# First batch's scores as float32 products from q and k, two heads in the rows' halves, and four pairs with float32 values instead of five

## The chip, the cores and the metric

The kernel runs on one core of one Trainium2 chip. The metric is device time in microseconds, the median of several executions. Engines are named as the profile names them: PE (TensorE matmuls), PEld (its weight loads), DVE (VectorE), ACT (ScalarE), POOL (GpSimd), and SP, whose queue issues the DMAs.

## The reference

Attention with a decay, and then a feed-forward layer, all in float32:

```
scores = q @ k.T / 8 + cum[query] - cum[key]      # cum: running sum of log f; causal mask
attn   = exp(scores - max);  attn /= sum(attn) + 1e-9
x      = attn @ v            # 8 batches, 8 heads, 576 positions, 64 wide
h      = x @ w_in;  out = (h * tanh(softplus(h))) @ w_out      # 4608 tokens, 512 -> 2048 -> 512
```

## The kernel before, in words

Two heads make a pair; there are 8 batches of 4 pairs, 32 pairs `g`. A chunk of the feed-forward layer takes 512 tokens: chunk `c` below 8 the first 512 positions of batch `c`, the ninth the 64 last positions of all batches. So the first chunk needs pairs 0 to 3 and, as it goes, the converted weights: `load_weights`, `convert_weights`, `scale_weights` and `split_weights` bring 32 blocks of w_in and w_out in and split each into an f16 high and low half.

Precision comes from such halves. `prep` (line 1060) scales q and k of a pair by a power of two found from their square sums (`square_sum`, on ACT), makes high halves (`scaled`) and low halves (`scaled_rest`) into a tile `hl`, and moves them by DMA into a stacked layout: `ST1` holds the 64 high rows of a head and under them six rows of decay sums with ones as partners, `ST2` high and low rows of the cross terms (`prep2`, line 1094). The constant rows of `ST1` are written at the start by `fill_rows` (line 755). A score is then two f16 products of up to 128 rows added in a PSUM bank. The decay sums are made once by `decay` (line 782) in three f16 parts, stored to DRAM (`cumd`) and read back for each pair.

Pairs below `NB` = 5 go one way, the later pairs another.

- Pairs 0 to 4: `max_items` makes the scores with queries as PSUM rows, from `ST1` alone, and DVE takes maxima of tiles; `fin` turns them by a transpose into rows `mr` (for pairs below `NSEL` = 4; pair 4 stores them into a row of `ST1` by DMA). `st_items` makes the scores again with keys as PSUM rows, in two passes, adds a mask product and, for pairs below 4, a product of a selector `sel` with `mr` that subtracts the maximum; ACT takes the exponential into f32 tiles. `pv_items` multiplies these by the f32 values `vf`, which hold a column of ones; `prep_v` scales v into them.
- Later pairs: `new_st_items` makes the scores once, with queries as rows, DVE adds the mask and finds the maximum, ACT takes the exponential, `turn` splits it into f16 halves (copy on ACT, difference on DVE) and turns them by a DMA transpose, and `new_pv_items` multiplies by f16 halves of v, three products a block.

Every operation is recorded in a `Program`, with `choose` where several engines could do it, and `beside` where products in different parts of the array go out together. `schedule` then lays down the order of each engine's queue from a cost for each operation (`cost`, line 262; `F32COL` for f32 products) and the dependences; `warmed` puts products into an unused bank where TensorE would be idle early. In the trace all of them stand under the line that records (L333), so rows are told apart by tiles and shapes. PSUM has seven banks for attention until pair 3 is done, then two.

Of the kernel before, what the change touches and what calls it, by code (L numbers as in the profile page):

```python
# [33 lines left out]
EXPMASK = 0x7F800000  # L34
LEAST = float(np.array([963 << 20], np.uint32).view(np.float32)[0])
KM = 71
MROW = 70
# [26 lines left out]
NSEL = 4  # L64
# [37 lines left out]
NB = 5  # L102
# [25 lines left out]
VTA = -1  # L128
# [32 lines left out]
class Program:  # L161
# [100 lines left out]
    def cost(self, eng, method, kw, aps):  # L262
# [421 lines left out]
def attn_moe(ctx: ExitStack, tc: tile.TileContext, qk, v, f, w_in, w_out, out):  # L684
# [7 lines left out]
    sp = Ring(ctx.enter_context(tc.tile_pool(name="sp", bufs=1)), pt=CH, hb=CH, me=CH, ot=CH)  # L692
# [54 lines left out]
    rowv = cp.tile([P, 2, 2], F16, name="rowv")  # L747
    for t, first, fills in ((0, 0.0, ((KM - 4, -1.0), (KM - 1, 0.0))), (1, 1.0, ((KM - 4, 0.0), (MROW, -MSC), (KM, 0.0)))):
        nc.gpsimd.memset(rowv[:, t], first)
        for row, x in fills:  # L750
            nc.gpsimd.affine_select(
                out=rowv[:, t], in_=rowv[:, t], pattern=[[0, 2]], compare_op=ALU.is_ge, fill=x,
                base=row - 1, channel_multiplier=-1)

    def fill_rows(t, e):
        for k in range(2):
            rows = t[D:P, :, k].bitcast(F32)
            one = ones[D:P, 0:96].unsqueeze(1).to_broadcast([D, 3, 96])
            for j in range(2):
                nc.choose(scaled(  # L760
                    rows[:, j].rearrange("p (a n) -> p a n", n=96), one, rowv[D:P, k].bitcast(F32), e))

    for t in ST1:
        fill_rows(t, "vector" if t is ST1[0] else "scalar")
# [5 lines left out]
    xat = xa[2]  # L770

# [10 lines left out]
    def decay():  # L782
# [8 lines left out]
        nc.vector.tensor_scalar(out=c[:, 0], in0=cm, scalar1=8.0, scalar2=None, op0=ALU.mult)  # L791
        nc.vector.scalar_tensor_tensor(
            out=r1, in0=cm, scalar=8.0, in1=c[:, 0], op0=ALU.mult, op1=ALU.subtract)
# [27 lines left out]
    def square_sum(o, x, scale=1.0):  # L821
        junk = sp.tile([P, S], BF16, name="junk", tag="junk", bufs=1)
        nc.scalar.activation(
            out=junk[:, 0 : x.shape[-1]], in_=x, func=AF.Square, scale=scale, accum_out=o)
# [22 lines left out]
    def all_sum(cols, name, least=2.0**-60):  # L847
        m = sp.tile([P, 1], F32, name="am_m", tag="am_m", bufs=4)
# [131 lines left out]
    def load_v(b, after=-1):  # L980
        vt[b] = []
        for p in range(NP):
            t = sp.tile([P, S], F32, name=f"v{b}_{p}", tag="v32", bufs=NV)
            if after >= 0:

                nc.gpsimd.tensor_copy(out=t[:, 0:1], in_=st[after]["hl"][:, 3, 0:1])
            nc.sync.dma_start(out=t, in_=v[b, p])
            vt[b].append(t)

    def amax_v(b):  # L990
        cols = sp.tile([P, NP], F32, name=f"vc{b}", tag="vc", bufs=4)
        for p in range(NP):
            square_sum(cols[:, p : p + 1], vt[b][p])
# [53 lines left out]
    def load_qk(g):  # L1047
        b, p = divmod(g, NP)
        if g in (2, 3):
            t = xa[(2, 0)[g - 2]].rearrange("p a h n -> p (a h n)").bitcast(F32)[:, 0 : 2 * S]  # L1050
# [6 lines left out]
    def place1(g):  # L1057
        return g % NST if g < NB else (g - NB + ((NB - 1) % NST == 0)) % 2

    def prep(g):  # L1060
        b, p = divmod(g, NP)
# [13 lines left out]
        if g in (1, 3):  # L1075
            hl = xa[1].rearrange("p a h n -> p (a h n)")[:, 0 : 4 * S].rearrange("p (t s) -> p t s", t=4)
        else:
            hl = sp.tile([P, 4, S], F16, name=f"hl{g}", tag="hl", bufs=NHL)
# [6 lines left out]
        nc.mark = f"rows{g}" if g < NSEL else None  # L1085
        for t in range(2):
            nc.sync.dma_start(out=ST1[i][D + 3 * t : D + 3 * t + 3, :, t], in_=cumd[h0 : h0 + 2].rearrange("h r s -> r h s"))
        nc.mark = None
        for j in range(2):
            nc.sync.dma_start(out=ST1[i][0:D, j], in_=hl[j * D : (j + 1) * D, 1:3])  # L1090
        if NSEL <= g < NB and g - NST >= NSEL:
            nc.sync.dma_start(out=ST1[i][MROW : MROW + 1, :, 0], in_=zrow[0:1])

    def prep2(g):
        hl = st[g]["hl"]
# [5 lines left out]
    def prep_v(g):  # L1101
        b, p = divmod(g, NP)
        vv = sp.tile([P, 9 * (D + 1)], F32, name=f"vv{g}", tag="vv")
        src = vt[b][p].rearrange("p (n d) -> p n d", d=D)
        if g < NB:
            vf = st[g]["vf"] = vv.rearrange("p (n d) -> p n d", d=D + 1)
            nc.gpsimd.memset(vf[:, :, D : D + 1], 1.0)
            nc.choose(*(scaled(vf[:, :, 0:D], src, vsc[b], e) for e in ("scalar", "vector", "gpsimd")))
            return
# [11 lines left out]
    if NB > NSEL + NST:  # L1121
        zrow = cp.tile([1, 2, S], F16, name="zrow")
        nc.gpsimd.memset(zrow, 0.0)

# [3 lines left out]
    def beside(*products):  # L1128
# [6 lines left out]
    sel = more_e.rearrange("p a n -> p (a n)").bitcast(F16)[:, 0 : 9 * P].rearrange("p (t k) -> p t k", t=9)  # L1135
    nc.vector.tensor_scalar(
        out=sel, in0=idm[:, 0:9].unsqueeze(2).to_broadcast([P, 9, P]), scalar1=-MSC / 1024.0, scalar2=None,
# [3 lines left out]

    def max_items(g):

        q1, k1 = ST1[place1(g)][:, :, 0], ST1[place1(g)][:, :, 1]
        s = st[g]
        KX = P

        def begin():

            s["mx"] = sp.tile([P, 20], F32, name=f"mx{g}", tag="mx", bufs=4)  # L1150
            nc.gpsimd.memset(s["mx"][:, 0:8:4], -3e38)

        def qk(o, j, t, k0, n, stop=True):
            q0 = t * P
            mm(o, q1[0:KX, j, q0 : min(q0 + P, S)], k1[0:KX, j, k0 : k0 + n], True, stop)
# [5 lines left out]
        def masked(c, ps, a, n, mb):  # L1161
            if g < GM:
                red(c, ps.rearrange("p (a n) -> p a n", a=a), a)
            else:
                d = sp.tile([P, a, n], F32, name=f"dg{g}_{c}", tag="ot", bufs=NOT)
                nc.vector.tensor_tensor(
                    out=d, in0=ps.rearrange("p (a n) -> p a n", a=a),
                    in1=mb.unsqueeze(1).to_broadcast([P, a, n]), op=ALU.add)
                red(c, d, a)

        def diag(j):
            ps = bank(f"md{j}_{g}")
            for t in range(4):
                qk(ps[:, t * P : (t + 1) * P], j, t, t * P, P, g >= GM)
                if g < GM:
                    mm(ps[:, t * P : (t + 1) * P], idm, msk, False, True)
            masked(10 + 4 * j, ps, 4, P, mskb)

        def t31(j):
            ps = bank(f"mt31{j}_{g}")  # L1180
            qk(ps[:, 0:384], j, 3, 0, 384)
            qk(ps[:, 384:512], j, 1, 0, 128)
            red(4 * j + 3, ps[:, 0:384])
            red(4 * j + 1, ps[:, 384:512])

        def t2():
            ps = bank(f"mt2_{g}")
            for j in range(2):
                qk(ps[:, 256 * j : 256 * j + 256], j, 2, 0, 256)
# [807 lines left out]
```

## Time and profile before

| | |
|---|---|
| median of 3 runs | 1017.91 us (1016.69 to 1018.59) |
| span of the profiled execution | 1012.6 us |
| the profiled execution's own time | not stated by the page; the median is 5.3 us above the span |
| PE, DVE, ACT busy | 978.1, 731.1, 728.9 us (97, 72, 72%) |
| chain that ended last | PE 65%, DVE 16%, ACT 7%, DMA 6% |

A busy PE is the union of its products' times, and the products are pipelined, so busy time is not work at the peak rate; what one product costs in a full queue is read from the distance between two starts. Each f32 product appears as two records.

### The profile page before, as it was taken

The numbers are of one execution on the slowest core, as the hardware profiler recorded it, in microseconds if no ns is written. First come the engines' busy times: TensorE is split into PE (matmuls) and PEld (weight loads), VectorE is DVE, ScalarE is ACT, GpSimd is POOL, SyncE is SP. The second block draws the span as 40 slices with busy tenths as digits, with TensorE's granted clock in tenths as the row PEclk, the third lists the DMA queues.
The fourth block names the chain that finished last, engine by engine and source line by source line (L and its number), as shares of the span: only waits on it lengthen the run. The fifth ranks groups of instructions, "written<-read, shape, count | busy, mean of one in ns | idle before, by whom it ended". The sixth has DMA issues, their size and how long they took to land.

```text
span 1012.6 us, 20652 instructions
## 1 busy us (share of the span) xinstructions
PE 978.1 (97%) x7663; PEld 544.1 (54%) x7663; DVE 731.1 (72%) x2002; ACT 728.9 (72%) x1421; POOL 10.4 (1%) x65
## 2 busy tenths in 40 slices
PE   4999899998999999999999999999999999999998
PEld 4788445544554554555455555455555555656664
DVE  7999999986677776776666766776766669953432
ACT  6668999978778777777778877787886665524323
POOL 2000000000000000000000000000000000000000
PEclk8999999999999999999999999999999999999999
DMA  6999974779777857687868766786775432001001
GB/s 198 324 266 244 262 169 108 154 173 187 158 145 160 173 127 153 136 180 145 142 141 179 148 146 142 170 158 115 138 152 112 70 75 72 4 1 42 1 1 42
DMA packets 256446, 139.57 MB, mean 138 GB/s; under 512 B 226650, under 2 KB 227034, under 8 KB 256346
## 3 DMA queue, kind: packets, MB, share of 16 engines
q1 hardware_dynamic: 256346, 138.26, 61.7%
q8 instruction: 60, 0.98, 0.4%
q14 instruction: 40, 0.33, 0.1%
HBM read 45.68 MB, written 9.66 MB: 55 GB/s over the span
## 4 chain that ended last, share of the span: by engine, by line
PE 65%; DVE 16%; ACT 7%; DMA 6%; issue 3%; SPq 1%; POOL 0%; DVEq 0%; ACTq 0%; POOLq 0%
PE b L333 65%; DVE wall L333 3%; DVE b L333 2%; DMA pt<-hb 2%; DMA st<-hl 2%; SPq L333 1%; ACT junk L333 1%; DVE hl L333 1%; DVE hb L333 1%; ACT st L333 1%; ACT hb L333 1%; DMA out_dram<-ot 1%; DVE gl L333 1%; DVE x L333 1%; ACT more_e L333 1%
## 5 line engine op out<-in xcount | busy, mean ns | idle before, releaser
L333 PEld LDWEIGHTS <-wall 128*128 128x128 f16 x3372 | 322.3, 98 | 357.9 <-issue 24.0
L333 PE MATMUL b<-gh,wall 128*128 128x512 f16 x1152 | 366.5, 380 | 0.0
L333 PE MATMUL b<-xa,wall 128*128 128x512 f16 (+1 forms) x1602 | 345.0, 366 | 8.3 <-ACT me L333 4.6
L333 PE MATMUL b<-gl,wall 128*128 128x512 f16 x576 | 218.2, 379 | 0.6 <-DVE gl L333 0.6
L333 PE MATMUL b<-st 70*128 70x512 f16 (+11 forms) x918 | 139.1, 285 | 13.7 <-DMA st<-cumd 6.9
L333 DVE SCALAR_TENSOR_TENSOR gl<-me,gsc,gh 128x512 f16<-128x512 f32 x144 | 106.3, 748 | 32.6 <-ACT gh L333 31.7
L333 ACT ACTIVATE me<-b,cinv 128x512 f32<-128x512 f32 (+1 forms) x130 | 85.0, 660 | 56.6 <-PE b L333 55.7
L333 PEld LDWEIGHTS <-st 70*128 70x128 f16 (+3 forms) x1110 | 87.3, 102 | 63.6 <-issue 18.7
L333 PE MATMUL b<-vv,pt 128*128 128x65 f16 (+5 forms) x2548 | 111.7, 203 | 1.1 <-DMA pt<-hb 0.7
L333 DVE CUSTOM_DVE_ANT_0 b<-b,mskw 128x256 f32<-128x256 f32 (+2 forms) x162 | 91.6, 567 | 9.9 <-PE b L333 8.8
L333 ACT ACT_TABLE_LOAD x70 | 89.8, 1283 | 1.2
L333 PEld LDWEIGHTS <-pt 128*128 128x128 f16 (+1 forms) x2268 | 70.9, 101 | 19.3 <-DMA pt<-hb 2.3
L333 ACT ACTIVATE st<-b,mn 128x512 f32<-128x512 f32 (+3 forms) x120 | 62.1, 548 | 22.7 <-DVE mn L333 19.4
L333 DVE TENSOR_TENSOR hb<-st,hb 128x512 f16<-128x512 f32 x81 | 55.8, 689 | 29.6 <-ACT hb L333 29.1
L333 DVE TENSOR_TENSOR hb<-more_e,hb 128x512 f16<-128x512 f32 x81 | 55.5, 689 | 29.6 <-ACT hb L333 29.3
L333 ACT ACTIVATE more_e<-b,mn 128x512 f32<-128x512 f32 (+3 forms) x123 | 62.4, 539 | 17.3 <-DVE mn L333 15.8
L333 DVE TENSOR_SCALAR gh<-me,gsc 128x512 f16<-128x512 f32 x66 | 31.9, 483 | 45.2 <-ACT me L333 44.3
L333 ACT ACTIVATE gh<-me,gsc 128x512 f16<-128x512 f32 x78 | 55.8, 720 | 1.8
L333 ACT ACTIVATE hb<-more_e 128x512 f16<-128x512 f32 x81 | 50.1, 627 | 9.5 <-DMA pt<-hb 8.8
L333 ACT ACTIVATE hb<-st 128x512 f16<-128x512 f32 x81 | 50.2, 627 | 7.6 <-DMA pt<-hb 5.6
L333 DVE TENSOR_TENSOR me<-b,hb 128x256 f32<-128x256 f32 x42 | 17.5, 422 | 50.5 <-PE b L333 49.9
L333 ACT ACTIVATE junk<-qk 128x576 bf16<-128x576 f32 x60 | 40.8, 680 | 15.5 <-DMA qk<-in_qk_dram 14.8
(173 smaller groups left out, 1005.3 us busy)
## 6 DMA issues: line engine op xcount, KB each, us to landing
st<-hl SPq DMA_DIRECT2D x180, 144.0 KB
qk<-in_qk_dram SPq DMA_DIRECT2D x30, 576.0 KB
v<-in_v_dram SPq DMA_DIRECT2D x32, 288.0 KB
out_dram<-ot SPq DMA_DIRECT2D x36, 256.0 KB
wall<-in_w_in_dram SPq DMA_DIRECT2D x16, 512.0 KB
wall<-in_w_out_dram SPq DMA_DIRECT2D x16, 512.0 KB
pt<-hb SPq DMA_TRANSPOSE x162
st<-xa SPq DMA_DIRECT2D x12, 144.0 KB
```

The costliest lines, as they stand in the source:

```text
L333: r = getattr(real[eng], method)(*a, **kw)
```

## The change

`NB` goes from 5 to 4, so pair 4 takes the later pairs' way. For pairs 0 to 3 there are no halves of q and k any more: the products take the loaded f32 q and k, whose two heads lie in rows 0 to 63 and 64 to 127, and put both heads' products side by side, each into a bank of its own. The decay term comes from `rk`, a tile with three rows of sums for each head, multiplied by ones; masks and maxima are added as f16 products of half height. For the 64 last queries of the maxima, `qz` holds q of both heads on the diagonal of a 128 x 128 block, and one product of full height does both. v is loaded straight into the f32 value tiles beside a ones column, unscaled; its scale moves into the reciprocal of the sums. `prep2`, `prep_v`'s scaling, `fill_rows` and the third `ST1` tile go.

The diff, cut to its core:

```diff
-KM = 71
-MROW = 70
+KR = D + 3
-NSEL = 4
-NB = 5
+NB = 4
...
                 m = int(out.shape[0])
-                n = max(F32COL * n * m / 128.0, 2.1 * m)
+                n = max(F32COL * n * m / 128.0, 2.1 * m) if rows > D else 4.2 * n
                 active = 0.44 * n
...
-    NST = 3
-    ST1 = [cp.tile([P, 2, 2, S], F16, name=f"st1_{i}") for i in range(NST)]
+    ST1 = [cp.tile([P, 2, 2, S], F16, name=f"st1_{i}") for i in range(2)]
...
-    for t in ST1:
-        fill_rows(t, "vector" if t is ST1[0] else "scalar")
+    rk = cp.tile([P, NB, S], F16, name="rk")
+    nc.gpsimd.memset(rk.rearrange("p g s -> p (g s)").bitcast(F32), 0.0)
...
     def load_v(b):
...
+            if b * NP + p < NB:
+                tag, n = ("v32", NV) if p < 2 else ("vv", 2)
+                t = sp.tile([P, 9 * (D + 1)], F32, name=f"v{b}_{p}", tag=tag, bufs=n)
+                t = t.rearrange("p (n d) -> p n d", d=D + 1)
+                nc.gpsimd.memset(t[:, :, D : D + 1], 1.0)
+                nc.sync.dma_start(out=t[:, :, 0:D], in_=v[b, p].rearrange("k (n d) -> k n d", d=D))
...
+    def prep_first(g):
+        h0, x = 2 * g, st[g]["qk"]
+        k = rk[:, g]
+        nc.mark = f"rows{g}"
+        for j in range(2):
+            nc.sync.dma_start(out=k[j * D : j * D + 3], in_=cumd[h0 + j])
+        nc.mark = None
+        z = qz(g)
+        for j in range(2):
+            r = slice(j * D, (j + 1) * D)
+            nc.gpsimd.tensor_copy(out=z[r, r], in_=x[r, 0, CH:S])
+
     def prep(g):
+        if g < NB:
+            prep_first(g)
+            return
...
     def max_items(g):
...
+        def scores(o, t, k0, n, tri=False):
+            q = slice(t * P, (t + 1) * P)
+            beside(*((o[j], x[r, 0, q], x[r, 1, k0 : k0 + n], True, False) for j, r in enumerate(HEADS)))
+            if tri:
+                for h in range(2):
+                    beside(*((o[j], (idm, idmx)[j ^ h][r], (msk, mskx)[j ^ h][r], False, False)
+                        for j, r in enumerate(HEADS)))
+            beside(*((o[j], one16[r], k[r, k0 : k0 + n], False, True) for j, r in enumerate(HEADS)))
...
         def t4a():
             ps = bank(f"mt4a_{g}")
-            for j in range(2):
-                qk(ps[j * D : (j + 1) * D], j, 4, 0, CH)
+            mm(ps, z, x[:, 1, 0:CH], True, False)
+            mm(ps, blk, k[:, 0:CH], False, True)
             red(8, ps)
...
     def st_items(g):
...
+        def block(o, k0, m, q0, n, tri=0):
+            ks = slice(k0, k0 + m)
+            beside(*((o[j], x[r, 1, ks], x[r, 0, q0 : q0 + n], True, False) for j, r in enumerate(HEADS)))
+            if tri and m == P:
+                for h in range(2):
+                    beside(*((o[j][:, h * D : (h + 1) * D], (msk, mskx)[j ^ h][r], idm[r, r], False, False)
+                        for j, r in enumerate(HEADS)))
+            elif tri:
+                beside(*((o[j], msk[r, r], idm[r, r], False, False) for j, r in enumerate(HEADS)))
+            for q in range(q0, q0 + n, P):
+                w = min(P, S - q)
+                tail = q == CH
+                beside(*((
+                    o[j][:, q - q0 : q - q0 + w], sel[r, 8 if tail else 4 * j + q // P, 0:m],
+                    s["mr"][r, r if tail else slice(0, P)], False, False)
+                    for j, r in enumerate(HEADS)))
+            ones_n = one16[:, 0 : min(n, P)]
...
+            beside(*((o[j], k[r, ks], ones_n[r], False, True) for j, r in enumerate(HEADS)))
...
+        def k2_():
+            ps = two("2")
+            block([o[:, 0:256] for o in ps], 2 * P, P, 2 * P, 256, P)
             for kt in range(4):
-                two_pass(ps[:, 256 + D * kt : 320 + D * kt], j, slice(kt * P, (kt + 1) * P), slice(CH, S))
-            finish(ps, f"T2{j}", CH, lambda e: tri(e, 1, P))
+                block([o[:, 256 + D * kt : 320 + D * kt] for o in ps], kt * P, P, CH, D)
+            finish(ps, "T2")
```

## Rows read from the trace of the kernel before

**Rows 1.** Stretches: length, busy (count) of PE, PEld, DVE, ACT, POOL, clock, DMA share.

```profile
0.00:20.00 20.00, 8.43 (x104) 8.19 (x105) 15.20 (x40) 14.27 (x29) 5.50 (x34) 0.88 0.57 180
20.00:40.00 20.00, 16.32 (x179) 12.35 (x176) 17.59 (x44) 11.21 (x25) 0.24 (x1) 0.87 0.99 310
40.00:100.00 60.00, 58.99 (x648) 50.13 (x648) 59.29 (x173) 45.54 (x114) 0.81 (x4) 1.00 1.00 266
100.00:200.00 100.00, 94.89 (x702) 48.58 (x701) 99.02 (x287) 97.53 (x174) 0.81 (x4) 0.98 0.75 174
...
300.00:500.00 200.00, 197.25 (x1597) 101.02 (x1596) 137.69 (x387) 153.62 (x298) 1.11 (x8) 1.00 0.75 154
860.00:1000.00 140.00, 140.00 (x902) 88.03 (x900) 70.92 (x146) 52.56 (x95) 0.00 (x0) 1.00 0.03 9
```

**Rows 2.** Groups of PE by form, 0 to 40 us: busy us, mean ns.

```profile
L333 PE MATMUL b<-idm,idh 128*128 128x128 f16 x133 | 12.2, 253 | 4.6 <-DVE idh L333 4.6
```

**Rows 3.** Waits up to 200 us: total, times, longest.

```profile
PE b L333 <- DMA st<-cumd: 6.9, 1, 6.9
```

**Rows 4.** Timeline of the opening: start us, length us, instruction.

```profile
2.02 1.79 DVE L333 TENSOR_SCALAR st<-ones,rowv 64x288 f32<-64x288 f32 x4 [0.36 <-POOL rowv L333]
2.09 3.48 ACT L333 ACTIVATE st<-ones,rowv 64x288 f32<-64x288 f32 x8
...
8.29 0.68 ACT L333 ACTIVATE junk<-qk 128x576 bf16<-128x576 f32 x1
...
11.00 0.71 SPq L333 DMA_DIRECT2D cumd<-st  x2
...
14.22 1.05 SPq L333 DMA_DIRECT2D st<-cumd  x3
...
18.51 0.27 PE L333 MATMUL b<-st 128*128 128x128 f16 x1 [6.94 <-DMA st<-cumd]
...
19.56 1.35 DVE L333 TENSOR_REDUCE mx<-b 128x4 f32<-128x512 f32 x3 [1.36 <-PE b L333]
```

**Rows 5.** Timeline of PE at full clock: merged products of one form.

```profile
38.11 0.33 PE L333 MATMUL b<-mr,more_e 128*128 128x128 f16 x3
...
39.40 1.53 PE L333 MATMUL b<-vv,pt 128*128 128x65 f32 x12
...
44.73 0.28 PE L333 MATMUL b<-vv,evs 128*64 128x65 f32 x2
...
44.94 0.23 PE L333 MATMUL b<-st 128*64 128x64 f16 x2
45.10 0.44 PE L333 MATMUL b<-vv,pt 128*128 128x65 f32 x2
...
57.66 0.36 PE L333 MATMUL b<-wsc,ones 128*128 128x4 f32 x2
...
338.60 0.57 PE L333 MATMUL b<-vv,pt 128*64 128x65 f16 x24
...
870.04 0.59 PE L333 MATMUL b<-gh,wall 128*128 128x512 f16 x2
```

**Rows 6.** Groups of PE by form, whole span.

```profile
L333 PE MATMUL b<-vv,pt 128*128 128x65 f32 x240 | 31.5, 277 | 0.0
```

**Rows 7.** Groups of DVE by form, 20 to 200 us.

```profile
L333 DVE SCALAR_TENSOR_TENSOR hl<-qk,qt,hl 128x576 f16<-128x576 f32 x10 | 8.0, 804 | 0.0
L333 DVE TENSOR_TENSOR hb<-more_e,hb 128x512 f16<-128x512 f32 x10 | 6.9, 688 | 0.0
L333 DVE TENSOR_REDUCE mx<-b 128x4 f32<-128x512 f32 x10 | 6.8, 679 | 1.5 <-PE b L333 1.5
```

**Rows 8.** Groups of ACT by form, 20 to 200 us.

```profile
L333 ACT ACTIVATE junk<-qk 128x576 bf16<-128x576 f32 x12 | 8.1, 679 | 1.1 <-DMA qk<-in_qk_dram 1.0
...
L333 ACT ACTIVATE hl<-qk,qt 128x576 f16<-128x576 f32 x7 | 5.3, 768 | 0.8 <-DMA st<-cumd 0.5 <-DVE qt L333 0.3
```

**Rows 9.** DMA issues, 0 to 100 us: count, KB of one.

```profile
st<-hl SPq DMA_DIRECT2D x25, 144.0 KB
```

More of the change, by code (lines that the diff above doesn't have):

```diff
@@ L34 @@
 EXPMASK = 0x7F800000
+ONE2 = float(np.array([0x3C003C00], np.uint32).view(np.float32)[0])
 LEAST = float(np.array([963 << 20], np.uint32).view(np.float32)[0])
-KM = 71
-MROW = 70
+KR = D + 3
 MSC = 2.0**10
@@ L738, in attn_moe @@
     nc.vector.memset(ones, 1.0)
-    NST = 3
-    ST1 = [cp.tile([P, 2, 2, S], F16, name=f"st1_{i}") for i in range(NST)]
+    ST1 = [cp.tile([P, 2, 2, S], F16, name=f"st1_{i}") for i in range(2)]
     ST2 = [cp.tile([P, 2, 2, S], F16, name=f"st2_{i}") for i in range(NST2)]
[L747 to L758, printed above, removed]
-            for j in range(2):
-                nc.choose(scaled(
-                    rows[:, j].rearrange("p (a n) -> p a n", n=96), one, rowv[D:P, k].bitcast(F32), e))
+    rk = cp.tile([P, NB, S], F16, name="rk")
+    nc.gpsimd.memset(rk.rearrange("p g s -> p (g s)").bitcast(F32), 0.0)
     for t in ST1:
-        fill_rows(t, "vector" if t is ST1[0] else "scalar")
+        nc.gpsimd.memset(t[D:KR, :, 0].bitcast(F32), ONE2)
     w_in, w_out = w_in.bitcast(I32), w_out.bitcast(I32)
@@ L1084, in prep @@
         h0 = b * H + 2 * p
[L1085 to L1088, printed above, removed]
+        nc.sync.dma_start(out=ST1[i][D:KR, :, 1], in_=cumd[h0 : h0 + 2].rearrange("h r s -> r h s"))
         for j in range(2):
             nc.sync.dma_start(out=ST1[i][0:D, j], in_=hl[j * D : (j + 1) * D, 1:3])
-        if NSEL <= g < NB and g - NST >= NSEL:
-            nc.sync.dma_start(out=ST1[i][MROW : MROW + 1, :, 0], in_=zrow[0:1])
     def prep2(g):
+        if g < NB:
+            return
         hl = st[g]["hl"]
@@ new lines, in fin, with st_items, two, finish @@
+            nc.tensor.transpose(out=ps, in_=mpad[:, g % 2], identity=idh)
+            mr = s["mr"] = sp.tile([P, P], F16, name=f"mr{g}", tag="mr", bufs=2)
+            nc.choose(*(scaled(mr, ps, None, e) for e in ("vector", "scalar")))
+        return [
+            (begin, 0), (diag, 900), (t31, 900), (t2, 450), (t4a, 1100), (t4b, 180), (fin, 60)]
+    def st_items(g):
+        x, k, s = st[g]["qk"], rk[:, g], st[g]
+        def block(o, k0, m, q0, n, tri=0):
[15 more added lines that the diff above has]
+            ones_n = one16[:, 0 : min(n, P)]
+            if n > P:
+                ones_n = ones_n.unsqueeze(1).to_broadcast([P, n // P, P])
+            beside(*((o[j], k[r, ks], ones_n[r], False, True) for j, r in enumerate(HEADS)))
+        def two(name):
+            return [bank(f"s{name}{j}_{g}") for j in range(2)]
+        def finish(ps, tag):
+            for j in range(2):
+                e = s[f"{tag}{j}"] = sp.tile([P, CH], F32, name=f"e{tag}{j}{g}", tag="pt", bufs=NPT)
+                nc.scalar.activation(out=e, in_=ps[j], func=AF.Exp, scale=0.125)
+        def k0():
+            ps = two("0")
+            block(ps, 0, P, 0, CH, P)
+            finish(ps, "T0")
+        def k13():
+            ps = two("1")
+            block([o[:, 0:384] for o in ps], P, P, P, 384, P)
+            block([o[:, 384:512] for o in ps], 3 * P, P, 3 * P, P, P)
+            finish(ps, "T1")
+        def k2_():
+            ps = two("2")
+            block([o[:, 0:256] for o in ps], 2 * P, P, 2 * P, 256, P)
@@ L1286, in k2_ @@
             for kt in range(4):
[L1287 to L1288 removed]
+                block([o[:, 256 + D * kt : 320 + D * kt] for o in ps], kt * P, P, CH, D)
+            finish(ps, "T2")
         def k4():
[L1291 to L1293 removed]
+            ps = two("4")
@@ L1538, in attn_moe @@
     rows = xat.rearrange("p a h n -> p (a h) n").bitcast(F32)
-    late = cp.tile([P, 704], F32, name="late")
     part = [
```

232 lines of the change are left out of this document (84 added, 148 removed).

## The prediction

> **What bounds the kernel now.** Read the run in stretches first [rows 1]. From 860 us TensorE is busy for all of 140 us, and from 300 to 500 us for 197.25 of 200: there the kernel is a queue of TensorE work, and nothing ends earlier unless that queue is shorter or was started sooner. The head differs. Up to 40 us TensorE is busy 8.43 + 16.32 = 24.75 us, and 12.2 us of that are warm-up products into an unused bank [rows 2], so useful products take 12.5 us and 27 us hold none; from 40 to 200 us another 1.0 + 5.1 us are idle. From 40 to 200 us VectorE is busy 59.29 of 60 and 99.02 of 100 us, ScalarE 97.53 of 100 after 100 us, and the DMA engines' share is 0.99 and 1.00 from 20 to 100 us. Three resources are full at once in the head, and TensorE has the slack.
>
> What opens it is read from the waits and the timeline. TensorE's longest wait is 6.9 us, put down to a DMA [rows 3]; it ends at 18.51 us with the first score product, and the first maximum is at 19.56 us [rows 4]. Before it come the decay sums (stored at 11.00 us, read back from 14.22 us), and the f16 high and low halves of q and k, which must be made on ScalarE and VectorE and moved by six DMAs a pair into the stacked layout. The raw q and k were there by 8.29 us, when ScalarE reads them.
>
> **TensorE work, part by part.** Prices are spacings of starts (busy time less one product's own length, over the number of gaps; the lengths 0.219, 0.38, 0.253, 0.277 and 0.222 us are those of single products of the form) [rows 5]: f16 128 columns (0.33 - 0.219)/2 = 0.056 us, 512 columns 0.59 - 0.38 = 0.21 us, and in proportion 0.162, 0.109 and 0.029 us for 384, 256 and 64. An f32 product shows as two records, each with its own weight load. With 4 columns they stand 0.36 - 0.253 = 0.11 us apart, with 65 columns (1.53 - 0.277)/11 = 0.11 us: at 128 weight columns the load sets the spacing. With 64 weight columns and 65 moving ones it is 0.28 - 0.222 = 0.058 us, so a moving column costs at most 0.0009 us a record. An f32 product then costs the larger of 0.22 us and 0.0018 us a column: 0.22 for 64 and 128, 0.46 for 256, 0.69 for 384, 0.92 for 512.
>
> *Removed, pairs 0 to 3.* Maxima: diagonals 16 x 0.056 = 0.90; 384 and 128 columns twice 0.44; 0.22; the last 64 queries 0.28; transpose 0.06: 1.90 us. Transposed scores, a head: 0.71 (512 columns in two passes, mask, four sums with the maxima), 0.77, 0.74, so 4.44 for two, 0.12 for the corner: 4.56. A pair: 6.46 us.
>
> *Added, pairs 0 to 3, if the two heads' products in rows 0-63 and 64-127 run at the same time.* f32 maxima: 4 x 0.22, 0.69 + 0.22, 0.46, and full-height 0.92 + 0.22 = 3.4; f32 transposed scores: 0.92, 0.91, 0.46 + 4 x 0.22, 0.12 = 3.3; masks, maxima and decay rows in f16: 1.34 + 1.88 = 3.2. A pair: 9.9 us, 3.5 us more; four pairs +13.9 us.
>
> *Pair 4.* Its f32 values go: 48 records of 128 weight columns (240 for five pairs) by 0.11 and, by the kernel's counts, 12 of 64 by 0.058 = 6.0 us [rows 5, 6]; so do its scores, 5.1 us (no sums with maxima there). The way of the later pairs costs, from the kernel's counts, scores 2.2 + 0.5 and 84 value products by 0.03 = 2.2: 4.9 us. That is -6.2 us.
>
> *Switches of the array's shape.* Two corner products in column halves begin at 44.94 us, 0.03 apart, and the next full-width product at 45.10: 0.13 us where 0.03 is usual [rows 5], so 0.1 us a switch. There will be more of them, as score products use half the height and value products all of it: between none and 50, 0 to 5 us. I take 2, as the order can gather products of one shape.
>
> Sum on TensorE: 13.9 - 6.2 + 2 = +9.7 us. The ends: no row shows products in row halves. The nearest rows are those in column halves: 24 products of 65 columns in 0.57 - 0.20 us, 0.016 us each, two at a time at 0.032 us a pair [rows 5]. I take the same for rows. If they ran one after the other, (5.6 + 2.7) us more a pair, +33 us in all, so +43 us.
>
> The Trainium skill (TensorE: Matmul & The Clock Gate, "Part 3: Packing small matmuls", measured speedups) gives 3.07 times for four products in row quarters, so packing is not free there; the column halves here show no loss. By its ratio the added work would be about 10 us dearer, which is rival 3.
>
> **What comes off the other engines.** VectorE loses the low halves of pairs 0 to 3, 8 x 0.804 = 6.4 us [rows 7], and the constant rows, 1.79 us [rows 4]; ScalarE four pairs' square sums (two of 0.679 us each) and one or two high halves of 0.768 us [rows 8], 8.5 us and more, 3.48 us of constant rows [rows 4] and the scaling of v. Pair 4's new way adds six low halves of 0.688 us on VectorE (4.1 us) [rows 7] and as many copies on ScalarE; its maxima read about 3,200 columns instead of 3,100, some 4.2 us by 0.679 for 512 either way. Net: VectorE -4 us, ScalarE about -8 us. On the DMA queue four pairs drop six 144 KB moves each, 3.5 MB of the 25 issues of the first 100 us [rows 9]; at the 310 GB/s of 20 to 40 us that is 11 us of a full resource, and weight loads queue up behind it, SP's issues included. The v loads now land in 256-byte pieces beside a ones column; the same bytes, hidden if they are there when the first values are wanted, which was at 39.40 us [rows 5]. The memsets and the block copies of q go to GpSimd, idle here except in the first 10 us.
>
> **When it starts.** Products need only q, k: 8.3 us instead of 18.51. With seven banks, pair 0's whole set of maxima fits, and each bank waits for the decay rows as its last term. Those come 2.5 us sooner if the decay takes the place of the constant rows, or no sooner; store to read-back is 3.2 us and landing about 2 more, so the first maximum is at 14 to 16.5 us, not 19.56. The wait for the moved halves of the next pairs goes entirely. After that a pair asks some 4.7 us of VectorE and 9.9 us of TensorE, so TensorE is what is late next.
>
> **The sum.** Useless time to 40 us falls from 27 us to about 15 (8.3 of waiting, 4 between there and the decay rows, 3 of lower clock; the grant is 0.88 and 0.87 in these stretches [rows 1]): -12 us. Between 40 and 200 us TensorE has 6 us of visible idle time [rows 1], and short gaps that the view closes; with lighter VectorE, ScalarE and DMA I take -6 of it. Against +9.7 that is -8.3 us. Crosscheck on VectorE: 4 us less work, begun 3 to 5 us earlier, in a stretch where it is full: -7 to -9. I take -8: a span of 1004.6 us after 1012.6. The page states no time of the profiled execution but its span; the median of the runs shown is 1017.91, 5.3 us above it, which I carry over: 1010.
>
> **Rivals.**
> 1. *Swallowed.* TensorE's early start comes back as waits for converted weights: VectorE full to 200 us speaks for it, the freed DMA and VectorE time against. Only VectorE's 4 us less work stays, and half of that goes to pair 4's longer chain: -2 us, 1016.
> 2. *The row halves do not overlap, or only their products do and not their weight loads.* This is the slower side. The place is pairs 0 to 3, 10 to 90 us. If only the loads follow one another, small blocks double: f32 +2.3 and f16 +1.3 us a pair, +15 us, 1025. If all does, +33 us, of which the head's slack hides about 15: 1028. It decides once a second head costs more than a fifth of the first, 8 us over four pairs. The column halves speak against it.
> 3. *Half-way overlap*, 1.5 products' work at a time instead of 2: 8.3 us a pair x 0.3 x 4 = +10 us, 1020, or 1018 with some hidden. That is the skill's ratio; the trace speaks against it as above.
> 4. *Lower clock.* Half-height f32 work keeps the grant at 1.2 GHz for two pairs: 20 us become 40, 12 of them in time unused before: 1018. For it: 0.88 and 0.87 at the start; against: 1.00 from 40 to 100 us with f32 values running.
>
> **How the numbers follow.** Forecast 0.58, rival 1 0.14, rival 2 0.14, rival 3 0.08, rival 4 0.06. About 2 us (0.2%) is what a measurement can tell, so "same" is 1015.9 to 1020. The forecast is faster nearly always, rival 1 in six of ten: 0.66. Same takes most of the rest of rivals 1 and 3 and part of rival 4: 0.14. Slower: rival 2 and what is left of 3 and 4, 0.20. The likeliest case's own range is 1003 to 1015; with rivals 1, 3, 4 and the cheaper end of rival 2 it is 1001 to 1026.
>
> **What would show it.** Right: the first score product near 8 us, the first maximum by 16.5 us, pairs of f32 products a few ns apart, 0.22 us for 128 columns of both heads, useless TensorE time to 40 us near 15 us, weight loads ending sooner, the stretch of full VectorE ending near 190 us. Wrong: f32 products of two heads 0.1 us or more apart, grant below 0.8 up to 60 us, or TensorE idle behind weight conversion after 90 us.

## The result and the profile after

The changed kernel takes 1025.73 us (median of five runs, 1021.73 to 1025.95) beside 1016.69 us for the kernel before in the same runs: ratio 1.0085, 95% interval 1.0057 to 1.0113. Forecast were 1010 us and faster; it is slower. The profiled execution of after has a span of 1023.6 us and took 1025.73 us, 2.1 us more; the runs of after lie in two groups, at 1021.7 to 1021.9 and at 1025.7 to 1026.0 us, so a difference of 4 us from its median is no more than its own spread.

The stretches of after, for comparison with [rows 1] (length, then busy time and count of PE, PEld, DVE, ACT, POOL, clock, DMA share):

```profile
0.00:20.00 20.00, 13.15 (x154) 10.82 (x155) 11.44 (x22) 3.55 (x4) 11.25 (x49) 1.00 0.61 182
20.00:40.00 20.00, 13.91 (x122) 8.61 (x121) 15.27 (x46) 10.98 (x31) 0.41 (x2) 0.83 1.00 364
40.00:100.00 60.00, 57.94 (x722) 48.18 (x720) 57.47 (x159) 41.85 (x104) 0.14 (x1) 1.00 0.78 241
100.00:200.00 100.00, 94.53 (x684) 48.90 (x683) 94.92 (x283) 92.76 (x159) 1.11 (x4) 0.95 0.68 147
```

ScalarE and the DMA engines are relieved as predicted (ACT 41.85 instead of 45.54 us from 40 to 100 us, DMA share 0.78 instead of 1.00). But VectorE, the engine that was full, is now idle by 2.5 and 5.1 us in the last two stretches, where it lacked 0.7 and 1.0 us before, and TensorE is no fuller.

TensorE's warm-up products of after up to 40 us (against [rows 2]) and its longest waits up to 200 us (against [rows 3]: total, times, longest):

```profile
L331 PE MATMUL b<-idm,idh 128*128 128x128 f16 x78 | 8.4, 285 | 2.8 <-DVE idh L331 2.8
```

```profile
PE b L331 <- DMA qk<-in_qk_dram: 4.0, 1, 4.0
PE b L331 <- DVE am_m L331: 3.1, 1, 3.1
...
PE b L331 <- DVE cols L331: 2.1, 1, 2.1
```

The opening on TensorE in after (start, length, instruction, idle time before it), against [rows 4]:

```profile
8.71 0.80 PE L331 MATMUL b<-qk 64*128 64x128 f32 x4 [4.04 <-DMA qk<-in_qk_dram]
...
11.90 3.20 PE L331 MATMUL b<-idm,idh 128*128 128x128 f16 x34
...
15.60 0.44 PE L331 MATMUL b<-qk 64*128 64x128 f32 x4
15.87 0.22 PE L331 MATMUL b<-msk,idm 64*128 64x128 f16 x1
15.88 0.27 PE L331 MATMUL b<-xa 64*128 64x128 f16 x2
15.93 0.22 PE L331 MATMUL b<-msk,idm 64*128 64x128 f16 x1
15.98 0.22 PE L331 MATMUL b<-rk,xa 64*128 64x128 f16 x2
16.04 0.44 PE L331 MATMUL b<-qk 64*128 64x128 f32 x4
...
24.21 0.38 PE L331 MATMUL b<-am_m,ones 128*128 128x1 f32 x2 [3.15 <-DVE am_m L331]
26.73 1.22 PE L331 MATMUL b<-qk,xa 128*128 128x512 f32 x1 [2.13 <-DVE cols L331]
```

The first score product stands at 8.71 us. A block of 128 by 128 scores of both heads, with four f32 records and six f16 products, recurs after 0.44 us. One after the other the f32 records alone would take 0.44 and the f16 products 0.34 us by the spacings of [rows 5], 0.78 us together; with full overlap it would be 0.39. So the row halves run together, at 0.05 us a block more than full overlap; in the trace the records of the two heads start 3 to 4 ns apart. The same stretch on VectorE, then on ScalarE and on SP's queue:

```profile
15.40 0.76 DVE L331 TENSOR_REDUCE mx<-b 128x1 f32<-128x256 f32 x2 [5.77 <-PE b L331]
...
23.82 0.16 DVE L331 TENSOR_REDUCE am_m<-vc 128x1 f32<-128x4 f32 x1 [2.61 <-ACT junk L331]
...
25.58 0.43 DVE L331 TENSOR_SCALAR wall<-wall 128x512 int32<-128x512 int32 x1 [1.42 <-DMA wall<-in_w_in_dram]
```

```profile
19.70 0.68 ACT L331 ACTIVATE junk<-v 128x576 bf16<-128x576 f32 x1 [12.76 <-DMA v<-in_v_dram]
...
23.01 0.68 ACT L331 ACTIVATE junk<-vv 128x576 bf16<-128x576 f32 x1
```

```profile
14.70 1.40 SPq L331 DMA_DIRECT2D v<-in_v_dram  x2
16.14 3.46 SPq L331 DMA_DIRECT2D vv<-in_v_dram  x2
19.65 2.63 SPq L331 DMA_DIRECT2D wall<-in_w_in_dram  x4
```

The maxima begin at 15.40 us, 4.2 us sooner than before. Then VectorE reaches the sum of v's squares (`am_m`), which waits for ScalarE, which waits for v; the four loads in 256-byte pieces hold SP's queue from 14.70 to 19.6 us. TensorE waits behind it (3.15 and 2.13 us, above), and the weights come behind it too: VectorE's first conversion, at 25.58 us, waited 1.42 us more for its block of w_in.

**Work and idle time of TensorE.** The useful work was worked out from the product records: each counts with the distance from its start to the next product's, but with no more than its shape needs in a full queue (spacings as in [rows 5]). What is left of the span is idle time, warm-up products and time lost at half clock, called idle below; time lost when the array changes its shape is in it too. These are one profile each, and the profiled execution is not always near the median: that of "before, four pairs" took 1026.5 us where its median is 1022.24, that of "after, v's sum constant" 1018.06 where its median is 1021.27. The draws, which lay down the same work in another order, are told of further on.

| kernel | span | work | idle | 0-40 | 40-120 | 120-260 | rest |
|---|---|---|---|---|---|---|---|
| before | 1012.6 | 932.7 | 79.9 | 29.9 | 12.0 | 11.4 | 26.6 |
| before, draw 0 | 1021.9 | 932.8 | 89.1 | 31.5 | 17.8 | 11.4 | 28.4 |
| before, draw 1 | 1017.2 | 932.6 | 84.6 | 31.2 | 10.3 | 13.7 | 29.5 |
| before, draw 2 | 1017.7 | 932.6 | 85.1 | 31.4 | 12.4 | 13.2 | 28.2 |
| before, draw 3 | 1027.3 | 932.7 | 94.6 | 32.0 | 19.0 | 12.4 | 31.2 |
| after | 1023.6 | 939.5 | 84.1 | 26.8 | 17.3 | 12.8 | 27.3 |
| after, draw 0 | 1023.0 | 939.0 | 84.0 | 27.4 | 15.8 | 11.2 | 29.6 |
| after, draw 1 | 1024.3 | 939.2 | 85.1 | 26.8 | 15.0 | 9.5 | 33.8 |
| after, draw 2 | 1030.4 | 938.7 | 91.7 | 27.4 | 16.2 | 17.6 | 30.5 |
| before, four pairs | 1024.8 | 926.6 | 98.2 | 30.4 | 23.9 | 16.3 | 27.7 |
| after, five pairs | 1025.7 | 949.0 | 76.7 | 26.7 | 10.3 | 9.9 | 29.8 |
| after, v's sum constant | 1016.3 | 939.1 | 77.2 | 21.5 | 18.2 | 9.5 | 28.1 |

### The profile page after: what moved, and what is told of

It reads as the page before. It is cut to its first block, busy times and chain, and to the rows that moved or that the text cites. A ratio compares the mean times of both kernels' runs of the same rounds, so it can differ in the third digit from the quotient of the medians.

```text
span 1023.6 us, 20891 instructions
## 1 busy us (share of the span) xinstructions
PE 989.9 (97%) x7838; PEld 547.7 (54%) x7838; DVE 737.2 (72%) x2018; ACT 712.4 (70%) x1350; POOL 16.1 (2%) x79
## 4 chain that ended last, share of the span: by engine, by line
PE 66%; DVE 17%; DMA 7%; ACT 5%; issue 3%; SPq 1%; POOL 1%; ACTq 0%; DVEq 0%; POOLq 0%
PE b L331 66%; DVE wall L331 4%; DVE b L331 3%; DMA pt<-hb 2%; DMA st<-hl 2%; DVE hb L331 2%; SPq L331 1%; DMA qk<-in_qk_dram 1%; DVE hl L331 1%; DMA wall<-in_w_out_dram 1%; ACT junk L331 1%; DVE x L331 1%; DVE gl L331 1%; ACT rk L331 1%; ACT more_e L331 1%
## 5 line engine op out<-in xcount | busy, mean ns | idle before, releaser
L331 DVE CUSTOM_DVE_ANT_0 b<-b,mskw 128x256 f32<-128x256 f32 (+2 forms) x168 | 95.3, 570 | 21.3 <-PE b L331 17.0
L331 PE MATMUL b<-st 128*128 128x384 f16 (+11 forms) x672 | 106.8, 299 | 2.6 <-ACT rk L331 1.3
L331 PEld LDWEIGHTS <-st 67*128 67x128 f16 (+3 forms) x864 | 68.9, 101 | 54.4 <-issue 16.9
L331 PE MATMUL b<-vv,pt 128*128 128x65 f16 (+3 forms) x2464 | 94.4, 199 | 3.5 <-DVE x L331 1.6
L331 ACT ACTIVATE more_e<-b,mn 128x512 f32<-128x512 f32 (+3 forms) x126 | 64.9, 543 | 37.5 <-DVE mn L331 33.5
L331 ACT ACTIVATE rk<-b,mn 128x512 f32<-128x512 f32 (+3 forms) x126 | 64.4, 543 | 24.2 <-DVE mn L331 22.7
L331 DVE TENSOR_TENSOR hb<-more_e,hb 128x512 f16<-128x512 f32 x84 | 57.7, 688 | 28.3 <-ACT hb L331 27.8
L331 DVE TENSOR_TENSOR hb<-rk,hb 128x512 f16<-128x512 f32 x84 | 57.4, 688 | 22.7 <-ACT hb L331 22.4
L331 ACT ACTIVATE hb<-rk 128x512 f16<-128x512 f32 x84 | 51.4, 625 | 4.2 <-DMA pt<-hb 2.3
L331 ACT ACTIVATE junk<-qk 128x576 bf16<-128x576 f32 x56 | 38.1, 680 | 19.7 <-DMA qk<-in_qk_dram 19.0
```

The source lines that it names most:

```text
L331: r = getattr(real[eng], method)(*a, **kw)
```

## The experiments

Diffs are against the kernel named. Each run's time is a median, its ratio is to the kernel before in the same runs, with its 95% interval.

**One part alone: four pairs, old start** (kernel before).

```diff
-NB = 5
+NB = 4
```

> The kernel before with four float32-value pairs instead of five; scores stay in f16 halves. Theory A (the loss sits in how v is now loaded and held: strided pieces, tiles taken until the value products end, and a TensorE sum of v that waits at the head of its queue): pair 4's move by itself takes 6 us of TensorE work off and puts 4 us on VectorE, so 1013 to 1019, no more than 2 us from before. Rival B (pair 4's way is what costs, in the stretch where VectorE is full): 5 to 9 us slower than before, 1022 to 1026.

Measured: 1022.24 us, ratio 1.0083 [1.0055, 1.0111], in rival B's range and as large a loss as that of after. The stretches of this kernel's trace from 88 us on:

```profile
88.00:92.00 4.00, 1.65 (x11) 0.77 (x10) 4.00 (x16) 2.58 (x6) 0.00 (x0) 1.00 1.00 278
92.00:96.00 4.00, 2.20 (x11) 0.91 (x10) 3.97 (x15) 4.00 (x14) 0.00 (x0) 1.00 1.04 289
96.00:100.00 4.00, 1.47 (x8) 0.59 (x5) 4.00 (x13) 3.90 (x12) 0.00 (x0) 0.94 1.08 280
100.00:104.00 4.00, 2.49 (x19) 2.01 (x20) 4.00 (x15) 3.19 (x7) 0.00 (x0) 0.50 0.98 139
```

TensorE is busy for 7.8 of 16 us, VectorE for 15.97 of them, and after the gap the granted clock is 0.50, which is 1.2 GHz. I took it for the cause that the f32 products of pair 4 no longer fill this stretch, until the draws below.

**How v is loaded** (changed kernel). First v whole, and copied beside the ones; then the planner told of a dearer load, so that it orders around it:

```diff
-                nc.sync.dma_start(out=t[:, :, 0:D], in_=v[b, p].rearrange("k (n d) -> k n d", d=D))
+            t = sp.tile([P, S], F32, name=f"v{b}_{p}", tag="v32", bufs=NV)
+            nc.sync.dma_start(out=t, in_=v[b, p])
...
+            nc.choose(*(scaled(vf[:, :, 0:D], src, None, e) for e in ("scalar", "vector", "gpsimd")))
```

> The changed kernel with v of the first pairs loaded whole into its ring and copied beside the ones column by ScalarE or VectorE (four copies of 0.8 us more), as the kernel before did, but unscaled. Theory A: the wait of SP's queue near 65 us (8 us) goes, the wait of TensorE near 21 to 27 us is shorter, weights land sooner, useless TensorE time up to 140 us falls by 6 us or more, and the time by 5 to 9 us, to 1016 to 1021. Rival B: no difference beyond 2 us, 1023 to 1027. Rival C (order of the queues is luck): moves by some us without those waits going.

Measured: 1026.27 us, 1.0101 [1.0069, 1.0134], in rival B's range. Of the two waits that should go, the one of SP's queue stayed: from 65.4 to 72.3 us SP stands before a load of v again, 6.9 us of it now for ScalarE's copies. The waits of TensorE behind v's sum did shrink, to 0.95 and 0.44 us, and the four loads held SP for 2.5 us instead of 4.9; yet the idle time to 40 us, worked out as in the table, is about 27 us as in after, since other waits came in their place (VectorE's maxima, 1.13 and 2.29 us).

```diff
+            if size == 4 * 128 * 576 and int(out.ap[-1][1]) == D:
+                return 1500 + DH, 4 * size / DRATE
```

> The changed kernel with the same strided loads of v, but the planner told that each takes four times the bytes' time and 1.5 us of issue, so that it lays out the queues for a late v. If the stall at 21 to 27 us comes from the order alone (the planner's belief), TensorE does pair 1's scores in it and the time falls by 3 to 6 us, to 1020 to 1023. If the loads and the held tiles themselves cost, it stays within 2 us of 1025.

Measured: 1022.01 us, 1.0076 [1.0055, 1.0098]. By the letter this is in the range for the order alone, but its ratio is within 0.001 of that of after, and their intervals overlap. Neither version gives the loss back.

**The changed kernel in another order** (draw 0), all work the same:

```diff
-NZ = 0
+NZ = 20
```

> The changed kernel with nothing changed in its work: the planner's first ranks get a random shift of up to 20 places, which gives another order of the same instructions. Rival C (order luck): the time moves by 4 us or more either way. Theories A and B: it stays within 3 us of 1025, and the waits near 21 and 65 us are there again in some form.

Measured: 1022.9 us, 1.0075 [1.0051, 1.0099], within the 3 us of theories A and B. The loss stays. What I did not see here is that only the same trial on the kernel before says what that means.

**Five pairs in the new way** (changed kernel), the second with the dearer load of v as well; the lines left out give pair 4 a copied v and a place among the decay rows, and move the next load of q and k:

```diff
-NB = 4
+NB = 5
...
-            mm(ps, z, x[:, 1, 0:CH], True, False)
+            mm(ps, z, s["qk"][:, 1, 0:CH], True, False)
```

> The changed kernel with five pairs by float32 products instead of four: pair 4 gets its six products of the float32 way back and loses its DMA transposes and its six low halves on VectorE. Theory D (the stretch to about 200 us is bound by VectorE, TensorE has time to spare there, so that pair 4's float32 way is work that fills TensorE at no price, while its later way is paid in VectorE time): about 8 us below the changed kernel, 1013 to 1018 us, and VectorE's busy time from 80 to 200 us lower than the changed kernel's. Rival (the loss is in the new start, its row halves, masks and waits): no faster than the changed kernel, 1022 to 1030 us.

> The same with the planner told of a four times dearer load of v in strided pieces, as in the earlier run with that price, so that the loads stand earlier in SP's queue. Theory D: as the five-pair form or 1 to 3 us below it, 1010 to 1017 us. Rival (start at fault): 1020 us or more.

Measured: 1027.09 us, 1.0105 [1.0063, 1.0148], and 1034.0 us, 1.0174 [1.014, 1.0208]. A miss for theory D; both are in the rival's ranges. In the first, idle time falls by 7.4 us against after (table), as theory D wanted, but the fifth pair is 9.5 us more TensorE work, and VectorE's busy time from 80 to 200 us is 116.55 us, not lower than the 112.79 of after. In the second the idle time does not fall either (about 84 us).

**More and less for VectorE and for the DMA transposes** (the first and the last on the kernel before, the two between on the kernel before with `NB = 4`):

```diff
-            nc.choose(*(sub(h[:, 1], e, h[:, 0], x) for x in LW_))
+            for _ in range(2 if g == NB else 1):
+                nc.choose(*(sub(h[:, 1], e, h[:, 0], x) for x in LW_))
```

> The kernel before with the six low halves of pair 5 made twice on VectorE: 4.1 us more VectorE time between 80 and 150 us and nothing else. Theory D (VectorE sets the end of this stretch): 3 to 5 us above the kernel before. Rival (DMA transposes and their place in SP's queue starve the weight loads, VectorE is not the limit): within 1 us of it.

Measured: 1018.9 us, 1.0029 [1.0011, 1.0047]: 4.8 us above the median of the kernel before and 2.9 by the ratio, about what theory D said.

```diff
+            if g == NB:
+                nc.gpsimd.memset(h[:, 1], 0.0)
+            else:
+                nc.choose(*(sub(h[:, 1], e, h[:, 0], x) for x in LW_))
```

> The kernel before with four pairs in float32 products, as in the first experiment, and with pair 4's six low halves of the attention weights set to zero on GpSimd instead of being worked out on VectorE (they are left out of the result): 4.1 us less VectorE time, all DMA transposes kept. Theory D: 3 to 4 us below the first experiment, about 1018 us. Rival (transposes): no change against the first experiment, 1021 to 1023 us.

Measured: 1022.36 us, 1.0078 [1.0057, 1.01]: no gain over the first experiment, as the rival said.

```diff
-            nc.choose(*(sub(h[:, 1], e, h[:, 0], x) for x in LW_))
+            if g != NB:
+                nc.choose(*(sub(h[:, 1], e, h[:, 0], x) for x in LW_))
...
+            if g == NB:
+                nc.gpsimd.memset(t[:, 4:8], 0.0)
+                nc.sync.dma_start_transpose(out=t[:, 0:4], in_=h[:, 0].rearrange("p (t n) -> p t n", n=P))
```

> The kernel before with four pairs in float32 products, as in the first experiment, and for pair 4 neither the low halves on VectorE nor their part of the DMA transposes (GpSimd writes zeros where they would land; they are left out of the result): 4.1 us less VectorE time and half of pair 4's transposed bytes. If pair 4's later way costs what it does by VectorE and transposes together: 3 to 5 us below the first experiment, 1017 to 1019 us. If it costs because TensorE has lost work that stood ready while nothing else did, and its clock falls: no more than 1 us below, 1021 to 1023 us, with TensorE again starved for several us between 80 and 120 us.

Measured: 1024.69 us, 1.0097 [1.0071, 1.0122]: less work, no gain, and above both ranges.

```diff
+            for _ in range(2 if g == NB else 1):
+                nc.sync.dma_start_transpose(out=t, in_=h.rearrange("p a (t n) -> p (a t) n", n=P))
```

> The kernel before with each DMA transpose of pair 5 issued twice: six more transposes between 85 and 150 us, no more work on any compute engine. If transposes and SP's queue hold the weight loads up: 3 us or more above the kernel before, 1017 us or more. If VectorE sets the pace there: within 1.5 us of it, 1013 to 1016 us.

Measured: 1025.03 us, 1.0098 [1.007, 1.0127]. By the letter this speaks for the transposes, and the run before it against them. Whichever way a few operations were moved, these four kernels are 3 to 11 us slower than the kernel before. That asked for a trial with no change of work.

**The sum of v's squares as a constant** (changed kernel):

```diff
+        if b == 0:
+            nc.gpsimd.memset(cols, float(S))
-        for p in range(NP):
+        for p in range(NP if b else 0):
```

> The changed kernel without the four square sums of the first batch's v: a constant stands in their place (the scale of the first batch's v is then not measured). VectorE's wait for the last of these sums at 21 us goes, and with it TensorE's 3.1 us wait behind it. If the early start of the new way is swallowed by this wait: 3 to 5 us below the changed kernel, 1018 to 1021 us, and VectorE busier between 10 and 40 us. If the DMA rate, full from 20 to 40 us, sets when weights can be converted anyway: within 1 us of the changed kernel, 1022 to 1026 us.

Measured: 1021.27 us, 1.0057 [1.0037, 1.0078], between the two ranges; its interval overlaps that of after. In the trace VectorE no longer stops for ScalarE after the first maxima, but it stops for the first block of w_in instead, and TensorE waits 3.50 us behind that where it waited 3.15 and 2.13:

```profile
16.64 4.00 DVE L331 TENSOR_REDUCE mx<-b 128x4 f32<-128x512 f32 x10 [6.48 <-PE b L331]
20.67 0.17 DVE L331 TENSOR_TENSOR mx<-mx 128x9 f32<-128x9 f32 x1
20.96 0.18 DVE L331 TENSOR_SCALAR mpad<-mx 128x18 f16<-128x18 f32 x1
24.85 0.43 DVE L331 TENSOR_SCALAR wall<-wall 128x512 int32<-128x512 int32 x1 [3.72 <-DMA wall<-in_w_in_dram]
```

```profile
26.76 1.89 PE L331 MATMUL b<-qk,xa 128*128 128x512 f32 x2 [3.50 <-DVE mx L331]
```

The first conversion of a weight moves only from 25.58 to 24.85 us. Idle time to 40 us is 5.3 us less than in after (table), in an execution that was the fastest of its five.

**Other orders of the same work.** A draw shifts the planner's first ranks at random, and the planner then lays all queues down again; it may also put some operations on another engine. Draw 0 of the kernel before is the edit shown above for the changed kernel; the further draws change SEED too:

```diff
-SEED = 122
-NZ = 0
+SEED = 1
+NZ = 20
```

> The kernel before with another draw of the planner's order, all work the same, as the earlier run did it for the changed kernel. If part of the difference between the two kernels is the order that the planner happened to find for the kernel before: 1017 us or more. If not: 1012 to 1016 us, within 2 us of the kernel before.

> The kernel before with a second draw of the planner's order, all work the same. Theory O (the order that the planner found without a draw is better than its orders commonly are): 1018 to 1026 us, as the first draw's 1023.2. Theory W (the work that the change moves makes the difference, and the first draw was a bad one): 1012 to 1017 us.

> The kernel before with a third draw. Theory O: 1018 to 1026 us. Theory W: 1012 to 1017 us.

> The kernel before with a fourth draw, all work the same. Theory O (its order without a draw is better than its orders commonly are): 1018 to 1026 us. Theory W (work makes the difference): 1012 to 1017 us.

Measured: 1023.22 us, 1.0077 [1.0057, 1.0098]; 1018.69 us, 1.003 [1.0011, 1.0048]; 1019.97 us, 1.0047 [1.0024, 1.0069]; 1028.99 us, 1.0152 [1.0125, 1.0179].

> The changed kernel with the same second draw. Theory O: 1018 to 1026 us, no further from the draws of the kernel before than these lie apart. Theory W: 1021 us or more, 6 us or more above the draws of the kernel before.

> The changed kernel with the same third draw. Theory O: 1018 to 1026 us. Theory W: 6 us or more above the draws of the kernel before.

> The kernel before with four pairs in float32 products, and the second draw of the order. Theory O: 1018 to 1026 us, among the draws of the kernel before, so that pair 4's move costs nothing that stands out of the spread of orders. Theory W: 6 us or more above the mean of the draws of the kernel before.

Measured: 1025.73 us, 1.0093 [1.0066, 1.0121]; 1030.62 us, 1.0144 [1.0097, 1.0191]; 1028.01 us, 1.0134 [1.0112, 1.0155].

Theory W, that the work makes the difference, falls for the kernel before: none of its four draws is within 1017 us, though the operations are the same. Theory O is met by two of the last three; the fourth draw is worse than it allowed. For the kernels with the changed work neither theory is borne out alone: the changed kernel's draw 1 is in theory O's range and 3.0 us above the mean of the draws of the kernel before, its draw 2 is above that range and 7.9 us above that mean, as theory W had it, and the kernel with four pairs, at 1028.01 us, is above the range of the one and, at 5.3 us above the mean, just short of the 6 us of the other. Where the draws lose is in one view, the first 120 us of each trace, columns as above. The kernel before, then draws 1, 2, 0 and 3:

```profile
0.00:120.00 120.00, 100.92 (x1029) 79.85 (x1030) 112.02 (x322) 90.25 (x200) 6.80 (x40) 0.96 0.94 263
0.00:120.00 120.00, 100.46 (x1064) 81.00 (x1065) 110.83 (x318) 91.69 (x201) 5.58 (x40) 0.94 0.89 250
0.00:120.00 120.00, 99.14 (x1029) 79.82 (x1030) 109.81 (x315) 89.42 (x196) 5.39 (x40) 0.94 0.95 260
0.00:120.00 120.00, 94.70 (x979) 77.40 (x979) 106.66 (x300) 86.18 (x193) 5.33 (x40) 0.93 0.86 246
0.00:120.00 120.00, 96.66 (x974) 79.95 (x974) 103.78 (x287) 84.36 (x197) 6.57 (x40) 0.90 0.89 251
```

VectorE has done 112.02, 110.83, 109.81, 106.66 and 103.78 us of work by then, and the spans are 1012.6, 1017.2, 1017.7, 1021.9 and 1027.3 us, in the same order. What VectorE has not done by 120 us it does later, and the end moves by more than that, in part because it has more to do: over the whole span it is busy 734.9 to 735.9 us in the draws and 731.1 us in the own order, as the planner put more on it. Five profiles in one order are a hint, not a test: nothing was tried that holds the order and moves VectorE alone, and the changed kernel's four orders (101.48 to 104.40 us by 120 us) do not line up so, nor does the kernel with four pairs in its own order, with 111.20 us by 120 us and a span of 1024.8.

## Why the prediction was wrong

**The step that failed is "The sum": useless TensorE time falling by 12 us to 40 us and by 6 after.** The start was predicted well, and TensorE's added work came out 2.9 us below its term. The idle time that was to pay for them did not fall by 18 us: over all orders of the two kernels it is 31.2 us before and 27.1 after up to 40 us, and 55.5 and 59.1 us from there on, so that nothing is left of the gain (86.7 and 86.2 us).

- *TensorE work, +9.7 us predicted.* Measured 939.5 - 932.7 = +6.8, within 0.8 of that in every draw. Pair 4 alone is 926.6 - 932.7 = -6.1 (predicted -6.2), so the new start is +12.9 (predicted 13.9, and 2 for switches, which this way of counting puts to the idle time and which no run measured).
- *Row halves.* They overlap, at 0.44 us a block where full overlap is 0.39; rivals 2 and 3 fall. By the Trainium skill's 3.07 times for four row quarters (TensorE: Matmul & The Clock Gate, "Part 3: Packing small matmuls") a block would take 0.51 us, an estimate from that figure; the trace shows less than half of that loss for two halves.
- *Clock.* Rival 4 falls: the granted clock is 1.00 up to 20 us and from 40 to 100 us, and 0.83 between, where TensorE stood for 5.3 us.
- *First product and first maximum.* 8.71 and 15.40 us for 8.3 and 14 to 16.5.
- *Useless time to 40 us, from 27 to 15.* By the view of the prediction it is 40 - (13.15 + 13.91 - 8.4) = 21.3 us: half of the gain. With products at half clock counted at their price it is 26.8 instead of 29.9, only 3.1 us less (table). What I left out is v. I had called its load in pieces "hidden if they are there when the first values are wanted, which was at 39.40 us". But the sum of v's squares is wanted at 21 us, in VectorE's queue ahead of the next maxima, and TensorE waits 5.3 us behind it (3.7 to 5.3 us in the three draws). With the sum gone, 5.3 us of idle time go, and by the view of the prediction 40 - (12.19 + 16.50 - 3.5) = 14.8 us are useless, the 15 that I had said; the kernel is still 0.57% slower than the kernel before. The sum is not the whole cause either: with v whole the waits behind it are 1.4 us and the idle time to 40 us is no less, and without the sum VectorE and TensorE wait for the first block of w_in. When those blocks can be there is a term that the prediction did not have.
- *Between 40 and 200 us, -6.* Visible idle time went from 6.1 to 2.06 + 5.47 = 7.5 us. The head start of VectorE was real: it had spent 37.96 us on converting weights (`wall`) by 80 us, against 27.99 before. From 80 to 120 us it spent 14.08 us instead of 20.36, and was idle for 4.84 us there instead of 0.76. The draws show the same on `wall`, 15.7 to 16.3 us in the changed kernel and 21.2 to 23.3 in the kernel before:

The kernel before, then after, VectorE's instructions on `wall` alone (length, busy and count, clock, DMA share):

```profile
0.00:40.00 40.00, 6.76 (x13) 0.87 0.78 245
40.00:80.00 40.00, 21.23 (x39) 1.00 1.04 286
80.00:120.00 40.00, 20.36 (x36) 1.00 1.01 259
```

```profile
0.00:40.00 40.00, 11.28 (x20) 0.91 0.81 273
40.00:80.00 40.00, 26.68 (x48) 1.00 0.71 242
80.00:120.00 40.00, 14.08 (x24) 0.87 0.84 196
```

SP's queue in after shows what may have come between; its longest wait from 60 to 100 us (total, times, longest) is for value products, 8.0 us, since v now stays in its loaded tile until they have read it:

```profile
SPq L331 <- PE b L331: 8.5, 2, 8.0
```

```profile
64.55 8.78 SPq L331 DMA_DIRECT2D v<-in_v_dram  x2
73.44 0.37 SPq L331 DMA_DIRECT2D wall<-in_w_out_dram  x1
```

A load of the second batch's v stands in the queue ahead of a weight load, and VectorE later waits 2.0 us for a block of w_out. TensorE then waits 1.6 us for VectorE, is busy for 2.96 of 4 us from 96 to 100 us, and goes on at half clock:

```profile
94.39 0.43 DVE L331 TENSOR_SCALAR wall<-wall 128x512 int32<-128x512 int32 x1 [1.99 <-DMA wall<-in_w_out_dram]
97.04 3.29 PE L331 MATMUL b<-vv,pt 128*128 128x65 f32 x26 [1.64 <-DVE x L331]
```

```profile
96.00:98.00 2.00, 0.96 (x9) 0.96 (x9) 2.00 (x8) 2.00 (x6) 0.00 (x0) 1.00 0.99 234
98.00:100.00 2.00, 2.00 (x19) 1.93 (x19) 2.00 (x6) 1.90 (x6) 0.00 (x0) 0.91 0.45 130
100.00:102.00 2.00, 2.00 (x13) 1.88 (x12) 2.00 (x7) 0.80 (x3) 0.00 (x0) 0.50 1.23 179
...
106.00:108.00 2.00, 2.00 (x6) 0.74 (x5) 1.46 (x5) 2.00 (x5) 0.00 (x0) 0.50 0.74 167
```

Four profiles of the changed kernel have 15.0 to 17.3 us of idle time between 40 and 120 us, so for the changed kernel this is not one bad order; but five of the kernel before have 10.3 to 19.0 us, so a larger idle time than before is not shown there, only that the 6 us did not go. That SP's queue holds the weights up was read, not tested: the version with v whole kept a wait of 6.9 us at the same place.

- *VectorE -4 us, ScalarE -8.* Measured over the whole span 737.2 - 731.1 = +6.1 and 712.4 - 728.9 = -16.5. By the means over all orders it is 734.5 - 734.4 = +0.1 and 711.7 - 726.1 = -14.4, since the planner places many operations on either engine: ScalarE was relieved by more than was said, VectorE not at all. Pair 4 was mis-sized: in the first experiment it adds 741.0 - 731.1 = 9.9 us to VectorE, and 742.5 - 735.9 = 6.6 us in the other order, where I priced 4.1 for its low halves alone.
- *The 5.3 us from span to time.* After took 2.1 us more than its span, and the other profiled executions 1.7 to 2.3, so by these some 3 us of the 5.3 were the distance of a fast execution from the median of three runs. The forecast is better judged by its span: 1004.6 us were said, 1023.6 measured.
- *Rival 1 (swallowed)* came nearest: the early start came back as waits, for v's sum and for the first blocks of w_in. It kept a gain of 2 us that was not there, and it left out that TensorE's added work then has to be paid: by the table's sums +6.8 of work and +4.2 of idle time are the 11.0 us between the two spans. These are the sums for the two submitted orders; over all orders it is +6.4 us of work and next to no change of idle time.

**What the result itself is worth.** The prediction also took for granted that the planner lays the changed work down as well as it did the old. The four draws of the kernel before take 1022.7 us on average, 7.8 us more than its own order in the runs beside them (about 1014.9). The changed kernel's four orders, the submitted one and three draws, take 1026.2. As ratios to the kernel before in the same runs these means are 1.0077 and 1.0099, 2.3 us apart with a standard error of 3.2 (from spreads of 0.54 and 0.31% over four orders each). A gain of 8 us is three standard errors away, but whether the change itself gains 4 us or costs 9 (two standard errors to either side) stays open. This leaves the own order of the kernel before out and takes that of the changed kernel in; with both in, the mean spans are 1019.3 and 1025.3 us, 6.0 apart with a standard error of 3.0. Shown are the +6.4 us of TensorE work (mean of four against mean of five), the idle time that does not pay for it (86.2 against 86.7 us, the same means), and an old order that is better than all its own draws. The first experiment's reading, pair 4 as the cause, is not shown: its 8 us are no more than a redraw costs. It is not excluded either, since both orders of that kernel have more idle time between 40 and 120 us (23.9 us, and about 21 in the other) than any of the five of the kernel before. Why the undrawn order of the kernel before is so good was not tried, nor whether a random shift by itself makes an order worse; the changed kernel's draws, at 1.0075, 1.0093 and 1.0144 after 1.0085 undrawn, do not settle it. No version tried beats the kernel before.

## What to carry to other kernels

Before a gain of idle time is counted, ask of each engine that is full what its next instruction waits for after the change; a measurement (here the sum of v) can be wanted long before the data itself. When a planner lays every queue down again, redraw the order of the kernel before with nothing changed, first of all: here that alone moved the time by 0.3 to 1.5%, as much as the change that was to be judged (0.85%). The work of the bound engine, added up product by product, is the steadier measure, since it stayed within 0.8 us over all orders of one kernel.

## What the hardware showed

f32 products in the two row halves run beside each other, with their weight loads: their records start 3 to 4 ns apart, and a block of two heads takes 0.44 us where one after the other would be 0.78 and full overlap 0.39. Four DMAs of v in 256-byte pieces held SP's queue 4.9 us (1.40 and 3.46 us for two each) and four of v whole 2.5 us, and for the kernel with v whole the time was no better.
